# Convolution groups of 16 channels in 8 segments instead of 24 channels in 5, with smaller blocks

## The chip, the core and the metric

The kernel runs on one core of one Trainium2 chip. The metric is device time in microseconds of one execution, lower is better. The engines are TensorE (PE, matmul; PEld is its weight load), VectorE (DVE), ScalarE (ACT), GpSimd (POOL) and SyncE (SP, which here only issues DMAs).

## What is computed

Input x is [8, 4224, 192] float32. First each of 8 heads of 24 channels is convolved causally along the sequence with 7 taps that are a softmax of that head's weights. Then a gated layer follows: a causal depthwise convolution with 5 taps per channel and a sigmoid give the gate, a 192x192 matmul gives the value, and their product goes through a second 192x192 matmul.

```python
out = einsum('hk,bskhg->bshg', softmax(weight), windows of 7 of x)      # x of the next part
gate_pre += conv_w[k] * xp[:, k:k + S, :]                               # k = 0..4
gate = 1 / (1 + exp(-gate_pre))
return gate * (x @ w_val) @ w_out
```

## The kernel before

The 8 sequences are laid end to end as two streams of 4, with padding between them. A step works on a block of the same positions in both streams. Each stream has 16926 positions (columns below), cut into 14 groups and these into 37 steps: 2 steps of 288, 6 of 432, 27 of 482, and a last group of 500 and 244.

**The first convolution** runs on TensorE, for whole groups of steps (`conv_unit`, lines 475 to 494). A window is 64 input positions (`HK`) that give 58 outputs (`HW`). The window's x is the stationary operand, 64 positions by the columns (segment, channel) of one head; the moving operand is the head's banded tap matrix `band`, 64 x 58. A head has 24 channels in 5 segments (`NS`), so M = 120 columns, cut into 64 and 56 (`cut`, line 97). Four matmuls make a pair of windows: two input halves (rows 0 to 63, 64 to 127) by two column halves. `NJS` (line 34) gives the pairs per head and group; in the text such a pair is called a window. Up to `UNIT` windows form a unit, which fills two PSUM banks; `evict` (line 496) has ScalarE copy each bank to the tile `e`, and `scatter` (line 520) then sends each finished head's rows with DMAs into the tiles x1 (channels of chunk 1, 128 of them, both streams side by side) and x2 (the other 64 channels, stream 0 on partitions 0 to 63, stream 1 on 64 to 127). Head h < 5 goes to x1 with one DMA, heads 6 and 7 go to x2 with two, and head 5 is split, with four.

```python
    for r, s in ((0, 0), (1, 1), (0, 1), (1, 0)):
        nc.tensor.matmul(pc[r][64 * s : 64 * s + c1 - c0, k * HW : (k + 1) * HW],
                         lhsT=xtiles[i][p, c + c0 : c + c1], rhs=band[p, 4 * q + hi, :], ...)
to = dst[:, : NS * (b - a)].rearrange("p (s t) -> p s t", s=NS)
dma(to[lo - c0 : hi - c0], e[p : p + NS * (hi - lo), a:b])     # dst is x1[h:120:5] for h < 5
```

**A step** then opens the gate's accumulators in PSUM on ScalarE (line 579: pa for x1, twice the columns; pb for x2), adds four taps to each on VectorE (line 597), and closes them with a sigmoid on ScalarE (line 610). x and the gated product are split into a high and a low part in float32r (`high` line 624, `low` line 629) for the two 192x192 matmuls: `main` (line 666, 128x128, three products), `rows` (line 686), and in plain f32 `columns` (line 695) and `diagonal` (line 653). In the last steps more of it is plain f32 (lines 659 and 678). VectorE multiplies value and gate (line 699; line 725 with a part left to GpSimd). Line 736 copies results to `ot`, and SyncE sends them out.

**Order.** Each engine runs its instructions in program order, and that order is written by hand in `ORDER` (line 116): one string per step whose tokens are the operations above, with +1 or -1 for the next or previous step. c1, c2, c3 are the conv units of the step, e10 to e31 their evictions (with the scatters behind the second), x one load of conv input (line 322) on SyncE's queue, mv/mo the mains, rv/ro the rows, cv/co the columns, dv/do the diagonals. The conv of a group runs two groups ahead of its use (`LAG`). Before the first string a prologue does groups 0 and 1 by other rules (lines 765 to 794). The loads have 8 buffers (`XBUFS`); a load brings 2 heads in small groups and 1 in large ones (`PER_LOAD`). Scatters of the first 3 groups to x2 are issued by GpSimd, two of group 0 by ScalarE, all others by SyncE.

Of the kernel before, what the change touches and what calls it, by code (L numbers as in the profile page):

```python
# [24 lines left out]
NS = 5  # L25
M = NS * HC
# [7 lines left out]
NJS = [2, 3, 3, 3] + [5] * 9 + [3]  # L34
# [10 lines left out]
def second(n):  # L45
    return NS * n * WIN - reach(n)

# [9 lines left out]
BLOCKS = {2: (288, 288), 3: (432, 432), 5: (482, 482, 482)}  # L57
# [3 lines left out]
TAIL = (500, LEFT - 500)  # L61
# [24 lines left out]
PERM = [h * HC + i for i in range(HC) for h in range(5)]  # L86
PERM += [5 * HC + i for i in range(8)]
PERM += [h * HC + i for i in range(HC) for h in (6, 7)]
PERM += [5 * HC + i for i in range(8, HC)]
QUADS = ((6, 7, 5, 0), (1, 2, 3, 4))  # L90
PER_LOAD = {2: 2, 3: 2, 5: 1}

EVEN = 99
SHARE = 241


def cut(g, h):
    return M // 2 if g >= EVEN and h < 5 else 64


UNIT = {2: 4, 3: 6, 5: 7}
# [3 lines left out]
BY_POOL, EARLY, AHEAD = 3, 4, 6  # L105
WARM = 11, 5, 14
# [10 lines left out]
    "rv xh2P+1 x x xl2+1 mv0 xhP+1 mv1 c1 x x x g0 e10 c2 xl+1 g1 A A e11 B A rv+1 dv cv e20 mv0+1 mv1+1 B A",  # L117
    """
    dv phP-1 xh2P+2 B g2-1 B e21-1 sA cv g0 pl-1 c1 g1 sB oA+1 e10 g2 do c2 do-1 e11 xh2+1 oB+1 e20 xh+1 e21 A
    A co co-1 mo0-1 mo1-1 x o2 xl2+2 B A ph o2-1 ph2-1 xl2+1 ph2P  # L120
    """,
    """
    dv A c3-1 B B B sA x x pl2-2 oA+1 cv pl-1 pl2-1 e30-1 e31-1 ro-2 c1 sB o0-2 A g2 A mo1-1 o1-2 mo0-1 oB+1
    e10 B ro-1 e11 rv ph2P o0-1 xh+1 x x xl c2 mv0 e20 o1-1 e21 A xl+1 mv1 B c3 xh2P+2 A sA+1 g0 oA+2 e30 B
    rv+1 g1 B mv1+1 mv0+1
    """,
    "dv do-1 A e31-1 sB xh+1 cv g0 A co-1 c1 x o2-1 oB+1 g2 g1 c2 xl2+1 pl2-1 phP-1 e10 x e11 e20 x x x pl-1",
    """
    dv do-1 ro-2 xl phP-1 ph2-1 e21-1 A B pl2-1 xh2P+1 A sA B B pl-1 oA+1 mo1-2 mo0-2 B o0-2 sB A cv c3-1 g2 A
    A A o1-2 e30-1 oB+1 e31-1 co-1 rv c1 e10 e11 o2-1 sA+1 mv0 mo0-1 mv1 B g0 g1 B mo1-1 xl2+1 xhP+1 ph2 xl+1  # L130
    phP ro-1 c2 oA+2 o1-1 A e20 e21 B do xhP+2
    """,
    """
    dv A B A A cv xh2+1 c3-1 co-1 e30-1 e31-1 rv sB x x o0-2 oB+1 B g2 o2-1 sA+1 mv1 mv0 B g1 pl-1 pl2-1
    xh2P+2 xl2+2 xhP+2 g0 B xl2+1 xl+1 oA+2 ph2P mo0-1 mo1-1 pl2 x x ro-1 o0-1 o1-1 do A
    """,
    """
    dv B A c1-1 e10-1 sB e11-1 co-1 ph-1 cv vp c2-1 e20-1 oB+1 pl-1 A A o2-1 gd mv0 x x e21-1 sA+1 mv1 x x
    oA+2 rv ro-1 gq B mo1-1 mo0-1 g1 B g0 do
    """,  # L140
    """
    dv o1-2 o0-2 B c1-1 co-1 A B cv e10-1 c2-1 sB e11-1 xh2+1 o2-1 xl mv0 vp oB+1 phP-1 e20-1 mv1 A A A xh+1
    pl-1 e21-1 gq ph2P-1 pl2-1 rv gd B sA+1 mo0-1 mo1-1 g0 c1 ro-1 B g1 ph2P pl2 xl2+1 oA+2 e10 e11 c2 o1-1 A
    ph e20 xl+1 B e21
    """,
# [57 lines left out]
    dv e11-1 x x ph-1 c2-1 xh2+1 co-1 e20-1 A A e21-1 x pl2-1 cv sB o2-1 ro-1 pl-1 vp gq rv gd A oB+1 B mv0  # L203
    mo0-1 g0 xh+1 mv1 B xl+1 g1 mo1-1 ph2P sA+1 o0-1 oA+2 B xl2+1 o1-1 c1 do e10 A B
    """,
    """
    dv e11-1 x ph-1 c2-1 xh2+1 co-1 e20-1 A A e21-1 x x pl2-1 cv sB o2-1 ro-1 pl-1 vp gq rv gd A oB+1 B mv0
# [7 lines left out]
    dv e11-1 x x ph-1 c2-1 xh2+1 co-1 e20-1 A A e21-1 x pl2-1 cv sB o2-1 ro-1 pl-1 vp gq rv gd A oB+1 B mv0  # L215
# [3 lines left out]
    dv e11-1 x ph-1 c2-1 xh2+1 co-1 e20-1 A A e21-1 x x pl2-1 cv sB o2-1 ro-1 pl-1 vp gq rv gd A oB+1 B mv0  # L219
# [4 lines left out]
    dv c2-1 co-1 cv o2-1 e20-1 rv pl-1 mv1 mv0 mo0-1 x x x vp e21-1 oB+1 gq gd xh+1 sA+1 g1 mo1-1 ph2P xl2+1  # L224
    pl2 c1 oA+2 e10 B ro-1 g0 B A e11 B xl+1 xh2P+2 o0-1 A
    """,
    """
    dv do-1 ph-1 o1-2 xh+1 c2-1 B e20-1 co-1 cv ro-1 e21-1 o2-1 sB vp oB+1 pl-1 gq rv A A mv0 mv1 B gd g1
# [4 lines left out]
    sA+1 x o0-1 gq B B gd mo1-1 o1-1 oA+2 x mv0 c1 xl+1 ph2P pl2 g1 g0 B e10 B A c2  # L233
# [6 lines left out]
    dv c1-1 cv B A B e10-1 e11-1 vt o1-2 sB oB+1 co-1 xl ro-1 rv A A gp B mo1-1 A o2-1 su+2 B mo0-1 o1-1 mv1  # L240
    mv0 g1 g0
# [20 lines left out]
def kernel(  # L262
# [30 lines left out]
    for g, n in enumerate(NJS):  # L293
        k = PER_LOAD[n]
        order = [h for q in QUADS for h in q]
        for i in range(0, NH, k):
            loads.append((g, order[i : i + k], o))
            o += WK * k * n * M
# [165 lines left out]
    for g, n in enumerate(NJS):  # L464
        for q in range(2):
            ws = [(hi, j) for hi in range(4) for j in range(n)]
            for i in range(0, len(ws), UNIT[n]):
                units.append((g, q, ws[i : i + UNIT[n]]))
    first_unit = [next(i for i, u in enumerate(units) if u[0] == g) for g in range(NG)] + [len(units)]

    def conv_unit(u):
# [479 lines left out]
```

## Time and profile before

| | |
|---|---|
| median of 3 runs | 346.68 us (346.58 to 348.18) |
| the profiled execution | 347.06 us |
| its span, granted clock | 345.3 us, 0.99 |
| busy: PE, DVE, ACT, POOL | 335.5, 316.2, 298.9, 284.4 us |
| DMA | 83.19 MB in 38947 packets, mean 241 GB/s |

The span runs from the first to the last instruction on record; the execution's own time is 1.8 us longer. A matmul's end is modelled, so PE's busy time overstates what the array does; what tells more is the chain that ended last, followed back from the end.

### The profile page before, as it was taken

The numbers are of one execution on the slowest core, as the hardware profiler recorded it, in microseconds if no ns is written. First come the engines' busy times: TensorE is split into PE (matmuls) and PEld (weight loads), VectorE is DVE, ScalarE is ACT, GpSimd is POOL, SyncE is SP. The second block draws the span as 40 slices with busy tenths as digits, with TensorE's granted clock in tenths as the row PEclk, the third lists the DMA queues.
The fourth block names the chain that finished last, engine by engine and source line by source line (L and its number), as shares of the span: only waits on it lengthen the run. The fifth ranks groups of instructions, "written<-read, shape, count | busy, mean of one in ns | idle before, by whom it ended". The sixth has DMA issues, their size and how long they took to land.

```text
span 345.3 us, 13001 instructions
## 1 busy us (share of the span) xinstructions
PE 335.5 (97%) x5334; PEld 215.0 (62%) x5334; DVE 316.2 (92%) x427; ACT 298.9 (87%) x543; POOL 284.4 (82%) x244
## 2 busy tenths in 40 slices
PE   8769999999999999999999999999999999999995
PEld 8755666666666666666666666666666764533343
DVE  4894999999999999999999999999999999999860
ACT  7564978688899999999999999999999999987752
POOL 1988699788999888988888988888989898974461
PEclk9996999999999999999999999999999999999999
DMA  7899969999897897797798897798899675421443
GB/s 265 261 217 280 251 207 285 267 278 321 235 307 270 254 292 257 236 285 265 223 276 284 244 279 274 221 275 285 261 277 324 216 254 153 155 70 56 173 173 132
DMA packets 38947, 83.19 MB, mean 241 GB/s; under 512 B 4936, under 2 KB 17008, under 8 KB 38888
## 3 DMA queue, kind: packets, MB, share of 16 engines
q1 hardware_dynamic: 37440, 80.64, 74.6%
q0 software_dynamic: 896, 1.27, 1.5%
q8 instruction: 42, 0.69, 0.9%
q10 hardware_dynamic: 552, 0.46, 0.4%
q14 instruction: 17, 0.14, 0.1%
HBM read 30.06 MB, written 26.00 MB: 162 GB/s over the span
## 4 chain that ended last, share of the span: by engine, by line
PE 93%; ACT 2%; DMA 1%; SPq 1%; DVE 1%; issue 1%; DVEq 0%
PE p L666 27%; PE p L695 18%; PE p L487 17%; PE p L686 14%; PE p L653 10%; PE p L678 3%; PE p L659 2%; PE p L375 1%; DMA x<-xw 1%; SPq L538 1%; ACT e L503 1%; DVE pa L597 1%; ACT g L610 0%; DVE pb L597 0%; ACT pa L579 0%
## 5 line engine op out<-in xcount | busy, mean ns | idle before, releaser
L597 DVE SCALAR_TENSOR_TENSOR pa<-x,cwt,pa 128x964 f32<-128x964 f32 (+4 forms) x148 | 173.2, 1170 | 2.4 <-ACT pa L579 0.7
L629 POOL TENSOR_TENSOR pl<-g,ph 128x482 fp32r<-128x482 f32 (+5 forms) x67 | 114.6, 1722 | 11.9 <-ACT ph L624 8.6
L629 POOL TENSOR_TENSOR xl<-x,xh 128x964 fp32r<-128x964 f32 (+5 forms) x62 | 98.0, 1584 | 17.1 <-ACT xh L624 12.4
L597 DVE SCALAR_TENSOR_TENSOR pb<-x,cwt,pb 128x482 f32<-128x482 f32 (+4 forms) x142 | 98.3, 692 | 0.7 <-ACT pb L579 0.2
L487 PEld LDWEIGHTS p<-band,x 64*56 64x56 f32 (+1 forms) x3776 | 67.7, 133 | 30.9 <-ACT e L503 8.9
L487 PE MATMUL p<-band,x 64*56 64x58 f32 (+1 forms) x3776 | 73.4, 220 | 4.8 <-issue 1.5
L503 ACT COPY e<-p 120x348 f32<-120x348 f32 (+2 forms) x148 | 63.3, 478 | 9.6 <-PE p L487 8.7
L736 ACT COPY ot<-p 128x482 f32<-128x482 f32 (+4 forms) x111 | 60.1, 550 | 11.7 <-PE p L695 4.0
L699 DVE TENSOR_TENSOR g<-p,g 128x482 f32<-128x482 f32 (+4 forms) x81 | 49.4, 620 | 12.7 <-PE p L695 4.4
L610 ACT ACTIVATE g<-pa 128x964 f32<-128x964 f32 (+4 forms) x37 | 34.8, 942 | 8.5 <-DVE pa L597 6.2
L624 ACT CAST xh<-x 128x964 fp32r<-128x964 f32 (+5 forms) x48 | 39.2, 818 | 0.0
L579 ACT ACTIVATE pa<-x,cwt 128x964 f32<-128x964 f32 (+4 forms) x37 | 38.4, 1037 | 0.7 <-DMA x<-xw 0.2
L653 PE MATMUL p<-g,wof 64*64 64x482 f32 (+4 forms) x148 | 37.3, 556 | 0.0
L653 PE MATMUL p<-x,wvf 64*64 64x482 f32 (+4 forms) x148 | 37.3, 569 | 0.0
L695 PE MATMUL p<-x,wvf 128*64 128x482 f32 (+4 forms) x148 | 36.5, 562 | 0.0
L695 PE MATMUL p<-g,wof 128*64 128x482 f32 (+4 forms) x148 | 36.1, 568 | 0.0
L624 ACT CAST ph<-g 128x964 fp32r<-128x964 f32 (+5 forms) x31 | 29.5, 950 | 0.0
L666 PE MATMUL p<-ph,woh 128*128 128x482 f32 (+4 forms) x74 | 28.8, 389 | 0.0
L624 POOL CAST ph<-g 128x482 fp32r<-128x482 f32 (+6 forms) x36 | 23.5, 653 | 6.2 <-DVE g L699 4.4
L666 PE MATMUL p<-xh,wvh 128*128 128x482 f32 (+2 forms) x64 | 27.5, 429 | 0.0
L666 PE MATMUL p<-pl,woh 128*128 128x482 f32 (+4 forms) x74 | 27.4, 370 | 0.0
L666 PE MATMUL p<-ph,wol 128*128 128x482 f32 (+4 forms) x74 | 27.4, 370 | 0.0
(79 smaller groups left out, 474.3 us busy)
## 6 DMA issues: line engine op xcount, KB each, us to landing
x<-xw SPq DMA_DIRECT2D x72, 300.0 KB
out<-ot SPq DMA_DIRECT2D x27, 723.0 KB
x<-e SPq DMA_DIRECT2D x45, 271.9 KB
x<-xw SPq DMA_DIRECT2D x16, 360.0 KB
x<-e SPq DMA_DIRECT2D x36, 135.9 KB
out<-ot SPq DMA_DIRECT2D x6, 648.0 KB
x<-e SPq DMA_DIRECT2D x20, 163.1 KB
x<-e SPq DMA_DIRECT2D x18, 90.6 KB
```

The source lines that it names most:

```text
L487: nc.tensor.matmul(pc[r][64 * s : 64 * s + c1 - c0, k * HW : (k + 1) * HW], lhsT=xtiles[i][p, c + c0 : c + c1], rhs=band[p, 4 * q + hi, :] ...
L503: nc.scalar.copy(ev[:, a : a + w, r, :], taken["c", u, r][:me, : w * HW].rearrange("p (w t) -> p w t", t=HW))
L579: nc.scalar.mul(acc, views(n, 0)[i], cwt[:, i, 0:1])
L597: nc.vector.scalar_tensor_tensor(out=acc, in0=views(n, k)[i], scalar=cwt[:, i, k : k + 1], in1=acc, op0=ALU.mult, op1=ALU.add,)
L624: copy(two[0], x)
L629: nc.gpsimd.tensor_tensor(out=l, in0=x, in1=h.bitcast(F32), op=ALU.subtract)
L653: nc.tensor.matmul(dst, lhsT=w22, rhs=x[HALVES[r]], start=True, stop=False)
L666: nc.tensor.matmul(acc, lhsT=a[:, r], rhs=b[:, q], start=(fresh and i == 0), stop=(not fresh and i == 2))
L686: nc.tensor.matmul(acc, lhsT=a[p, r], rhs=b[p], start=(fresh and i == 0), stop=(not fresh and i == 2))
L695: nc.tensor.matmul(acc[HALVES[q if what == "v" else 1 - q]], lhsT=w.f[:, W12 : W12 + 64], rhs=x[:, q], start=False, stop=True)
L699: nc.vector.tensor_tensor(out=v, in0=drop("v", n, q), in1=v, op=ALU.mult)
L736: nc.scalar.copy(ots[n][:, q * m : (q + 1) * m], drop("o", n, q))
```

## The change

The 192 channels are put in the order of `HEADS` and cut into 12 groups of 16 channels. A group has 8 segments, so M = 2 x 8 x 8 = 128: its two column halves have 64 columns each, 8 channels by 8 segments, and each half lies in one head, so it has its own `band`. The first 4 groups are chunk 2, the other 8 chunk 1. Group g's channels lie on every 8th partition of x1, or on every 4th of x2, and the weights' rows are permuted to match. A chunk 1 group is scattered with one DMA of 16 channels x 8 segments, a chunk 2 group with two. `NJS` falls to 1, 2 and 3, and the blocks become 230, 462 and 462, with a last group of 482, 482 and 256, 38 steps in all. All units have 6 windows; there are 74 of them, as before. Loads bring 3 groups at once in the small groups and 2 in the large ones, 76 loads instead of 92. In `ORDER` the x tokens are placed anew, most behind an eviction, there is one more string of the steady form, and near the end the unit c2 with its evictions is added in one string; all else stands.

```diff
-NS = 5
-M = NS * HC
+NS = 8
+OCT = 8
+M = 2 * OCT * NS
-NJS = [2, 3, 3, 3] + [5] * 9 + [3]
+NJS = [1, 2, 2, 2] + [3] * 10
-BLOCKS = {2: (288, 288), 3: (432, 432), 5: (482, 482, 482)}
+BLOCKS = {1: (230, 230), 2: (462, 462), 3: (462, 462, 462)}
-TAIL = (500, LEFT - 500)
+TAIL = (482, 482, LEFT - 964)
-PER_LOAD = {2: 2, 3: 2, 5: 1}
+HEADS = (6, 7, 5, 0, 1, 2, 3, 4)
+CHANNELS = [h * HC + i for h in HEADS for i in range(HC)]
+PLACES = [range(g, C2, 4) for g in range(4)] + [range(g, 128, 8) for g in (0, 4, 1, 5, 2, 6, 3, 7)]
+PER_LOAD = {1: 3, 2: 3, 3: 2}
-UNIT = {2: 4, 3: 6, 5: 7}
+UNIT = {1: 6, 2: 6, 3: 6}
...
-    dv e11-1 x x ph-1 c2-1 xh2+1 co-1 e20-1 A A e21-1 x pl2-1 cv sB o2-1 ...
+    dv e11-1 x ph-1 c2-1 xh2+1 co-1 e20-1 A A e21-1 x pl2-1 cv sB o2-1 ...
...
-            two = ((0, cut(g, h)), (cut(g, h), M))
             for r, s in ((0, 0), (1, 1), (0, 1), (1, 0)):
-                p, (c0, c1) = HALVES[r], two[s]
+                p = HALVES[r]
                 nc.tensor.matmul(
-                    pc[r][64 * s : 64 * s + c1 - c0, k * HW : (k + 1) * HW],
-                    lhsT=xtiles[i][p, c + c0 : c + c1],
-                    rhs=band[p, 4 * q + hi, :],
+                    pc[r][HALVES[s], k * HW : (k + 1) * HW],
+                    lhsT=xtiles[i][p, c + 64 * s : c + 64 * s + 64],
+                    rhs=band[p, (2 * h + s) * OCT // HC, :],
...
-        if g < BY_POOL and h >= 5:
+        if g < BY_POOL and h < SMALL:
             dma = nc.gpsimd.dma_start
-        elif g == 0 and h in (3, 4):
+        elif g == 0 and h in BY_ACT:
...
+        def send(dst, a, b):
+            dma(dst[:, : NS * (b - a)].rearrange("p (s t) -> p s t", s=NS), e[:, a:b])
+
+        at = PLACES[h]
+        if h >= SMALL:
+            send(x1[at.start : at.stop : at.step], 0, r)
         else:
+            for i, (a, b) in enumerate(((0, hf), (r - hf, r))):
+                send(x2[64 * i + at.start : 64 * i + at.stop : at.step], a, b)
```

## Rows read from the trace of the kernel before

**Rows 1.** The page: busy us (share of the span) and instructions of each engine.

```profile
PE 335.5 (97%) x5334; PEld 215.0 (62%) x5334; DVE 316.2 (92%) x427; ACT 298.9 (87%) x543; POOL 284.4 (82%) x244
```

**Rows 2.** The chain that ended last: shares of the span by line.

```profile
by line: PE p L666 27.4%; PE p L695 18.5%; PE p L487 16.9%; PE p L686 13.5%; PE p L653 9.8%; PE p L678 3.5%; PE p L659 2.4%; PE p L375 1.4%; DMA x<-xw 1.2%; SPq L538 0.9%; ACT e L503 0.8%; DVE pa L597 0.7%; issue 0.6%; ACT g L610 0.3%; DVE 
```

**Rows 3.** The same chain in order of time: start us, us, what.

```profile
178.41 0.91 PE p L487 x46
...
180.19 0.82 PE p L487 x49
181.01 1.77 PE p L695 x8
182.78 1.63 PE p L686 x12
184.41 2.81 PE p L666 x12
187.22 0.83 PE p L487 x39
188.06 0.83 PE p L653 x7
188.89 0.81 PE p L487 x46
...
195.84 0.91 PE p L487 x47
```

**Rows 4.** Busy us by stretch: the early one, then one steady group of three steps.

```profile
core 0: us, PE busy (x) PEld busy (x) DVE busy (x) ACT busy (x) POOL busy (x), PEclk, DMA share, GB/s
...
20.00:40.00 20.00, 18.11 (x310) 11.33 (x308) 15.41 (x26) 12.68 (x26) 15.21 (x21) 0.83 0.93 244
...
222.25:248.43 26.18, 26.18 (x444) 17.72 (x447) 25.93 (x34) 25.70 (x46) 23.30 (x19) 1.00 0.91 275
```

**Rows 5.** Conv matmuls by shape, whole span: count, busy us, mean ns of one.

```profile
L487 PE MATMUL p<-band,x 64*64 64x58 f32 x1888 | 72.5, 223 | 2.3 <-DMA x<-xw 1.0 <-ACT e L503 0.6 <-ACT pa L579 0.6
...
L487 PE MATMUL p<-band,x 64*56 64x58 f32 x1888 | 66.3, 218 | 2.5 <-issue 1.5 <-ACT e L503 0.8
```

**Rows 6.** TensorE's timeline, successive 128x128 matmuls: start us, us.

```profile
21.09 0.30 PE L666 MATMUL p<-xh,wvh 128*128 128x288 f32 x1
...
21.36 0.29 PE L666 MATMUL p<-xl,wvh 128*128 128x288 f32 x1
...
150.16 0.38 PE L666 MATMUL p<-xh,wvh 128*128 128x482 f32 x1
...
151.25 0.38 PE L666 MATMUL p<-pl,woh 128*128 128x482 f32 x1
```

**Rows 7.** VectorE's taps by shape, and two of them in the timeline.

```profile
L597 DVE SCALAR_TENSOR_TENSOR pa<-x,cwt,pa 128x964 f32<-128x964 f32 x108 | 131.9, 1221 | 1.7 <-ACT pa L579 0.5
...
L597 DVE SCALAR_TENSOR_TENSOR pa<-x,cwt,pa 128x576 f32<-128x576 f32 x8 | 6.5, 817 | 0.1
...
161.68 1.22 DVE L597 SCALAR_TENSOR_TENSOR pa<-x,cwt,pa 128x964 f32<-128x964 f32 x1
162.81 0.71 DVE L597 SCALAR_TENSOR_TENSOR pb<-x,cwt,pb 128x482 f32<-128x482 f32 x1
```

**Rows 8.** The timeline of the start; brackets: idle time before, and what ended it.

```profile
20.95 0.65 ACT L610 ACTIVATE g<-pa 128x576 f32<-128x576 f32 x1 [2.00 <-DVE pa L597]
...
30.49 0.46 DVE L699 TENSOR_TENSOR g<-p,g 128x288 f32<-128x288 f32 x1 [3.56 <-PE p L695]
...
32.06 0.98 ACT L579 ACTIVATE pa<-x,cwt 128x864 f32<-128x864 f32 x1 [0.23 <-DMA x<-xw]
```

**Rows 9.** DMA queues (SyncE's, ScalarE's): packets, MB, share; and SyncE's scatter issues, ns.

```profile
q1 hardware_dynamic: 37440, 80.64, 74.6%
...
q10 hardware_dynamic: 552, 0.46, 0.4%
...
L538 SPq DMA_DIRECT2D x<-e x158: 586/777/1638, 8.4 to 306.3; - x158
```

More of the change, by code (lines that the diff above doesn't have):

```diff
@@ L82 @@
 XC = NS * fifth(NMAX)
[L86 to L90, printed above, removed]
-PER_LOAD = {2: 2, 3: 2, 5: 1}
-EVEN = 99
+HEADS = (6, 7, 5, 0, 1, 2, 3, 4)
+CHANNELS = [h * HC + i for h in HEADS for i in range(HC)]
+C2 = D - 128
+GROUPS = D // (2 * OCT)
+SMALL = C2 // (2 * OCT)
+PLACES = [range(g, C2, 4) for g in range(4)] + [range(g, 128, 8) for g in (0, 4, 1, 5, 2, 6, 3, 7)]
+PERM = [0] * D
+for _g, _p in enumerate(PLACES):
+    for _i, _a in enumerate(_p):
+        PERM[_a + (128 if _g < SMALL else 0)] = CHANNELS[2 * OCT * _g + _i]
+HALF = GROUPS // 2
+PER_LOAD = {1: 3, 2: 3, 3: 2}
 SHARE = 241
-def cut(g, h):
-    return M // 2 if g >= EVEN and h < 5 else 64
-UNIT = {2: 4, 3: 6, 5: 7}
+UNIT = {1: 6, 2: 6, 3: 6}
 XBUFS, EBUFS = 8, 3
@@ L105 @@
 BY_POOL, EARLY, AHEAD = 3, 4, 6
+BY_ACT = GROUPS - 2, GROUPS - 1
 WARM = 11, 5, 14
@@ L294 @@
         k = PER_LOAD[n]
-        order = [h for q in QUADS for h in q]
-        for i in range(0, NH, k):
-            loads.append((g, order[i : i + k], o))
+        for i in range(0, GROUPS, k):
+            loads.append((g, range(i, i + k), o))
             o += WK * k * n * M
@@ L465 @@
         for q in range(2):
-            ws = [(hi, j) for hi in range(4) for j in range(n)]
+            ws = [(hi, j) for hi in range(HALF) for j in range(n)]
             for i in range(0, len(ws), UNIT[n]):
@@ L885 @@
     flat[:, pre : pre + SEQS * PADB].reshape(ns, SEQS, PADB, D)[:, :, :S] = x.reshape(ns, SEQS, S, D)
-    order = [h for q in QUADS for h in q]
+    chunk1, chunk2 = CHANNELS[C2:], CHANNELS[:C2]
     xw, base = [], 0
     for g, n in enumerate(NJS):
-        c = 5 * HC
         win = np.empty((NS * n, 2, HK, D), f)
@@ L897 @@
                 q += base + r * fifth(n)
-                win[w, i, :, c:] = flat[t, q : q + HK, c:]
+                win[w, i, :, :C2] = flat[t, q : q + HK, chunk2].T
         base += TOKS[g]
-        win = win[:, :, ::-1].reshape(NS, n, WK, NH, HC)
-        for i in range(0, NH, PER_LOAD[n]):
-            part = win[:, :, :, order[i : i + PER_LOAD[n]]]
+        win = win[:, :, ::-1].reshape(NS, n, WK, GROUPS, 2 * OCT)
+        for i in range(0, GROUPS, PER_LOAD[n]):
+            part = win[:, :, :, i : i + PER_LOAD[n]]
             xw.append(part.transpose(2, 3, 1, 4, 0).ravel())
     perm = np.array(PERM)
-    taps = weight[order, ::-1]
+    taps = weight[list(HEADS), ::-1]
     bw = np.full((2, HK, NH, HW), -1e30, f)
```

143 lines of the change are left out of this document (63 added, 80 removed).

## The prediction

> **What bounds the kernel now.** I read the page's first parts, then the chain that ended last, then three steady stretches, then single instructions. The page [rows 1] shows three engines near full, TensorE 97%, VectorE 92%, ScalarE 87%, so an average cannot say which one paces. The chain [rows 2] can: nearly all of it is TensorE, and line 487, the convolution, holds 16.9% of 345.3 us, 58.4 us. In order of time [rows 3] the pieces of a step follow each other without a gap: conv, f32 matmuls, rows, mains, conv again. A steady group of three steps takes 26.18 us and TensorE is busy for all of it, VectorE for 25.93, ScalarE for 25.70, the DMA engines for 0.91 [rows 4]. So TensorE paces, with VectorE close behind; a stage gains only by what TensorE's chain loses, and only until VectorE stops it. The exception is the start: there VectorE sits idle for 3.56 us until a TensorE result comes, step 2 opens at 32.06 us [rows 8], and TensorE, after waiting again and again, runs from 20 to 40 us at a mean granted clock of 0.83 [rows 4], so part of that stretch at the lower of its two levels (1.2 and 2.4 GHz).
>
> **The change, part by part.**
> *Convolution windows.* One window is 8 matmuls: two input halves, two column halves, and each f32 matmul runs as two instructions. Before there are 59 windows for each of 8 heads, 472 (3776 matmuls [rows 5] over 8); after, 1 + 3 x 2 + 10 x 3 = 37 for each of 12 groups, 444. The four column and row tiles of a window run side by side, one column half 64 wide and one 56 wide before, both 64 wide after. Does the fuller half cost? The 64-wide matmuls are busy for 72.5 us and the 56-wide for 66.3, equal counts [rows 5]: the narrow tiles finish early and the wide ones set the end, before as after. So a window keeps its price. That price has three readings: 58.4 us over 472 is 0.124 us; conv falls from 0.91 + 0.82 to 0.83 + 0.81 where a step has 13 windows rather than 14 [rows 3], 0.09 us; and the two steps' lengths, 8.81 and 8.62 us from conv to conv, differ by 0.19. I take 0.124, the mean over all of them. Removed: 28 x 0.124 = 3.5 us (2.5 to 5.3), all on the chain. The Trainium skill (TensorE: Matmul & The Clock Gate, LDWEIGHTS) says that a weight load takes time by its columns alone. By the total of columns, 472 x 120 against 444 x 128, that would leave nothing of these 3.5 us and the sum would be +1.4; no run here shows yet whether the column halves load one after the other, and the busy times above speak against it.
>
> *One more step.* Columns in all are the same 16926, cut into 38 steps, not 37, most of 462 columns, not 482. What counts is the part of a step that does not go by columns. Successive 128x128 matmuls start 0.218 us apart at 482 columns (150.16 to 151.25, five of them) and 0.135 apart at 288 (21.09 to 21.36, two) [rows 6]: 0.428 ns a column. A step has 12 passes on line 666 and 6 pairs on line 686; on line 695 eight f32 instructions lie two abreast in 1.77 us [rows 3], 0.44 each, so each counts two passes, 8 in all, and line 653's, four abreast, 4. 30 passes are 12.8 ns a column. A steady step is 26.18 / 3 = 8.73 us; less 482 x 12.8 ns = 6.17 and 13.33 x 0.124 = 1.65 leaves 0.9 us for drains and switches. The added step costs 0.9 us (0, if all went by columns, to 1.45, VectorE's fixed part below).
>
> A steady group then takes 26.18 - 4 x 0.124 - 60 x 12.8 ns = 24.91 us for 1386 columns: 17.97 ns a column against 18.11.
>
> *VectorE and ScalarE.* VectorE's fused tap costs (1221 - 817) / 388 = 1.04 ns per element [rows 7] and a column of a step has 14.5 elements there (four taps of two, four of one, two and a half gate products): 15.1 ns. Its 25.93 us become 25.93 - 60 x 15.1 ns = 25.02, which is more than 24.91. But busy time hides slack: a tap of 1.22 us is followed after 1.13 [rows 7], so each instruction starts up to 0.09 us before the last ends. Start to start, a step is 4 x 1.13, 4 x 0.62 (the 0.71 us tap less 0.09), and an estimated 1.44 for the three gate products by the same slope: 8.4 us, 25.3 a group, and 24.4 after. I count nothing for it; if that slack is not to be had, it is the first rival. ScalarE's evictions stay 148, and 72 of them get 348 columns instead of 406; they lie beside TensorE, on an engine at 25.70 of 26.18 us a group, and shrink with it.
>
> *Scatters.* 13 per group become 16, 182 become 224 in all; loads 92 become 76. ScalarE's queue shows how many engines a scatter uses: 552 packets [rows 9] are two band loads of 128 rows plus 16 closing packets and two scatters of 120 rows plus 12. So 24 channels x 5 segments go over 12 engines while loads go over 16; 16 channels x 8 segments should go over 16. Rows get shorter (2320 to 1392 B, 1160 to 696), packets rise by about 8100. By the count, 8100 x 110 ns (74.6% of 16 engines over 37440 packets) would be 56 us per engine; by bytes nothing. The short packets of ScalarE's queue (40 ns for 0.83 KB, against 110 for 2.15 KB [rows 9]) show that cost goes by bytes, so I count near nothing. SyncE issues 40 scatters more at 0.78 us [rows 9] and 16 loads fewer, GpSimd two more; SyncE has the room, 123 us of 345 for scatters now (158 x 0.777). The loads also move in the written order, most to behind an eviction, so on SyncE's queue they come after that eviction's scatters; their eight buffers hold 16 groups of 12, not 8 heads of 8, so each may come later in its group and I count nothing. The conv of a group runs two groups ahead, some 50 us, and this hides both in steady state; without that cover a wait for a landing would stand at once in the chain, where the loads now have 1.2%.
>
> *The start.* Group 0 shrinks from 576 to 460 columns. If step 2 opens when it does now, the 116 missing columns must be done later at 18.1 ns: +2.1 us. Against it: step 0's taps are shorter by 4 x 0.12 + 2 x 0.06 = 0.6 us, and group 1's last eviction waits for them through ScalarE's order (2.00 us of idling at 20.95 [rows 8]); group 0's conv has 4 windows fewer, 0.5 to 0.7 us; and group 1's scatters leave over more engines. I take +0.5 us, between +2.1 and -0.7, nearer the middle since both the data and VectorE's wait on TensorE come earlier.
>
> *Sum.* -3.5 + 0.9 + 0.5 = -2.1 us against the profiled execution's 347.06 us (span 345.3 and 1.8 around it), 345.0; the median of runs is 0.4 lower, so 344.6 us. A difference of 0.5% (1.7 us) is about what a measurement here can tell from none.
>
> **Rivals.**
> *VectorE paces.* Place: every steady step. For it: 25.93 of 26.18 us busy, and 25.02 against TensorE's 24.91 after. Against: the chain holds next to no VectorE now, and the overlap above. If VectorE keeps the idling it has, a step costs 8.73 - 482 x 15.1 ns = 1.45 us beside its columns, conv gains nothing, and the added step costs 1.45: with the start, 346.68 + 1.45 + 0.5 = 348.6 us, slower. It decides once VectorE's unavoidable time per 462-column step exceeds 24.91 / 3 = 8.30 us (I have 8.1).
>
> *Weight loads share one path.* Then conv goes by columns, 58.4 us stays, and 346.68 + 0.9 + 0.5 = 348.1 us: no change. Against it, rows 5.
>
> *The start gives it back.* Group 1's data is no earlier, the debt of 2.1 us stands: 346.68 - 3.5 + 0.9 + 2.1 = 346.2 us, no change. For it: ScalarE waits a last 0.23 us for a DMA at 32.06 [rows 8], so the data is only just in time.
>
> *The clock.* A mean of 0.83 over 20 us [rows 4] is 6.8 us at the lower level, so 3.4 us lost. If shorter waits at the start keep the clock up all the way, 344.6 - 3.4 = 341.2 us; nothing in the rows says that the waits shrink so far.
>
> *The scatters still use 12 engines.* Then nothing in the sum moves.
>
> **How the numbers follow.** The forecast has 0.55 (own range 342.8 to 346.4), VectorE 0.12, the loads 0.09, the start 0.14, the clock 0.10. Faster by over 0.5% means below 344.95: two thirds of the forecast and the clock, 0.47. Slower, above 348.4, most of VectorE's case and a little beside, 0.13. Between, 0.40. The range reaches from the clock's 341.2 to VectorE's 348.6.
>
> **What would show it.** In the profile after: 3552 matmuls on line 487, all 64*64, and conv of some 1.5 us a step, the same 0.12 us a window (right), or 0.13 and up (loads share a path). Steady groups of 24.9 us with TensorE full; if they take 25.2 or more and TensorE idles before conv or rows on VectorE, the first rival holds. Step 2 should open near 30.5 us; at 32 the start has given back its part. ScalarE's queue should show 2 x (128 + 16) twice, 576 packets. The prediction is wrong if conv's share of the chain does not fall, or if waits for the scattered tiles appear in it.

## The result, and the profile after

The changed kernel takes 349.95 us (median of 14 runs, 347.65 to 350.87) against 346.63 us before (14 runs, 344.5 to 349.11). The ratio is 1.0074, 95% interval [1.0048, 1.0100]: 2.6 us slower, where 2.1 us less were predicted. The profiled execution took 349.12 us, its span 347.3. A second series gave 1.0053 [1.0015, 1.0091] (run e16). Times below are ratios to the kernel before, measured on the same chip, times 346.6 us. The ratios leave out every run that took over 1.5% more than the fastest of its kernel; of the six of e8 below these are four, the profiled one among them.

Line numbers have moved: conv is now line 491 (487 before), eviction 506 (503), scatter 534 (538), x loads 327 (322), taps 587 (597), sigmoid 600 (610), f32 columns 685 (695), mains 656 (666).

First the page's engine line, the chain by line, one steady group of the chain in order of time (start us, us, what), and the busy times of the early stretches and of that group. They answer to [rows 1 to 4].

```profile
PE 332.5 (96%) x5150; PEld 215.6 (62%) x5150; DVE 316.8 (91%) x438; ACT 297.0 (86%) x554; POOL 287.6 (83%) x252
```

```profile
by line: PE p L656 26.1%; PE p L685 17.2%; PE p L491 14.4%; PE p L676 12.8%; PE p L643 9.3%; DMA x<-xw 5.2%; PE p L668 3.4%; PE p L649 2.4%; DVE pa L587 1.6%; DMA x<-e 1.3%; SPq L534 0.9%; issue 0.7%; ACT g L600 0.7%; DVE pb L587 0.6%; SPq 
```

```profile
201.86 0.85 PE p L491 x48
...
203.50 0.69 PE p L491 x48
...
210.16 0.85 PE p L491 x48
...
211.80 0.69 PE p L491 x48
...
218.45 0.85 PE p L491 x48
...
220.13 0.79 PE p L491 x45
```

```profile
20.00:40.00 20.00, 17.05 (x345) 11.42 (x335) 14.58 (x26) 11.98 (x26) 12.89 (x21) 0.83 0.87 237
40.00:60.00 20.00, 18.17 (x328) 11.68 (x330) 18.98 (x25) 15.90 (x32) 17.69 (x15) 1.00 0.77 219
201.86:226.79 24.93, 24.93 (x413) 17.20 (x415) 24.82 (x34) 24.54 (x46) 22.82 (x19) 1.00 0.93 271
```

The first 60 us in one line, the sum of three stretches of 20:

```profile
sum 60.00, PE 49.27 PEld 36.29 DVE 46.88 ACT 39.50 POOL 42.63; mean PE 16.42 PEld 12.10 DVE 15.63 ACT 13.17 POOL 14.21
```

The steady group is what the prediction said: 24.93 us (24.91 forecast), TensorE full, VectorE at 24.82 just under it. The chain shows what is new in this profile: loads of x have gone from 1.2% to 5.2% of it, 4 us to 18 us. A landing of scattered rows, which the prediction named as a sign of being wrong, is in it too (1.3%, a single piece of 4.51 us at 9.85 us); the second profile's chain has no such piece. The third stretch and the same sum of the kernel before (columns as in [rows 4], whose second stretch belongs between) tell where (a second profile of each kernel, in e5 and e16 below, shows how much of it stands):

```profile
40.00:60.00 20.00, 19.85 (x394) 13.14 (x394) 19.32 (x26) 16.82 (x35) 18.81 (x17) 1.00 0.83 252
sum 60.00, PE 53.98 PEld 39.54 DVE 48.70 ACT 42.21 POOL 46.17; mean PE 17.99 PEld 13.18 DVE 16.23 ACT 14.07 POOL 15.39
```

TensorE was busy for 53.98 of the first 60 us before and for 49.27 after: 4.7 us more of idling. The granted clock is the same, a mean of 0.83 in the second stretch, so part of it at the lower level in both. The DMA engines are not busier but idler (0.77 against 0.83 in the third stretch), so it is not that they are full. Here are the changed kernel's waits of TensorE for loads (total us, times, longest), three of them in TensorE's timeline, and the opening of step 2 on ScalarE, which answers to [rows 8]:

```profile
PE p L491 <- DMA x<-xw: 7.7, 7, 1.6
```

```profile
23.06 0.92 PE L491 MATMUL p<-band,x 64*64 64x58 f32 x48 [1.19 <-DMA x<-xw]
...
25.59 1.55 PE L491 MATMUL p<-band,x 64*64 64x58 f32 x48 [1.61 <-DMA x<-xw]
...
54.81 0.92 PE L491 MATMUL p<-band,x 64*64 64x58 f32 x48 [1.27 <-DMA x<-xw]
```

```profile
31.49 1.03 ACT L569 ACTIVATE pa<-x,cwt 128x924 f32<-128x924 f32 x1 [0.22 <-DMA x<-xw]
```

Step 2 opens at 31.49 us, hardly before the 32.06 of [rows 8], with 116 columns less done; the prediction wanted 30.5. (In the second profiles it is 30.80 and, before, 30.59.) The load that TensorE awaits at 54.81 us is issued as late as 50.55 us, between scatters, as SyncE's timeline shows:

```profile
47.65 2.84 SPq L534 DMA_DIRECT2D x<-e  x4
50.55 1.71 SPq L327 DMA_DIRECT2D x<-xw  x2
```

Last, the rows that answer to [rows 5, 9]: conv by shape, the two queues, and SyncE's scatter issues (ns min/median/max).

```profile
L491 PE MATMUL p<-band,x 64*64 64x58 f32 x3552 | 68.7, 222 | 9.5 <-DMA x<-xw 7.7 <-ACT e L506 1.8
```

```profile
q1 hardware_dynamic: 45648, 81.01, 78.2%
...
q10 hardware_dynamic: 576, 0.36, 0.4%
```

```profile
L534 SPq DMA_DIRECT2D x<-e x198: 532/592/2571, 7.7 to 299.1; - x198
```

All 3552 matmuls are 64*64, ScalarE's queue has the 576 packets that the prediction named as the sign of scatters over 16 engines, and a scatter's issue is shorter than before (medians 0.59 us against 0.78).

### The profile page after: what moved, and what is told of

Same layout as the page of the kernel before. It is cut to its first block, busy times and chain, and to the rows that moved or that the text cites. A ratio compares the mean times of both kernels' runs of the same rounds, so it can differ in the third digit from the quotient of the medians.

```text
span 347.3 us, 12737 instructions
## 1 busy us (share of the span) xinstructions
PE 332.5 (96%) x5150; PEld 215.6 (62%) x5150; DVE 316.8 (91%) x438; ACT 297.0 (86%) x554; POOL 287.6 (83%) x252
## 3 DMA queue, kind: packets, MB, share of 16 engines
q1 hardware_dynamic: 45648, 81.01, 78.2%
## 4 chain that ended last, share of the span: by engine, by line
PE 85%; DMA 7%; DVE 2%; ACT 2%; SPq 2%; issue 1%; ACTq 0%
PE p L656 26%; PE p L685 17%; PE p L491 14%; PE p L676 13%; PE p L643 9%; DMA x<-xw 5%; PE p L668 3%; PE p L649 2%; DVE pa L587 2%; DMA x<-e 1%; SPq L534 1%; ACT g L600 1%; DVE pb L587 1%; SPq L327 1%; ACT e L506 1%
## 5 line engine op out<-in xcount | busy, mean ns | idle before, releaser
L587 DVE SCALAR_TENSOR_TENSOR pa<-x,cwt,pa 128x924 f32<-128x924 f32 (+3 forms) x152 | 174.1, 1145 | 3.2 <-ACT pa L569 1.4
L619 POOL TENSOR_TENSOR pl<-g,ph 128x462 fp32r<-128x462 f32 (+4 forms) x69 | 115.3, 1682 | 12.4 <-ACT ph L614 9.1
L619 POOL TENSOR_TENSOR xl<-x,xh 128x924 fp32r<-128x924 f32 (+2 forms) x64 | 99.3, 1556 | 14.9 <-ACT xh L614 13.8
L587 DVE SCALAR_TENSOR_TENSOR pb<-x,cwt,pb 128x462 f32<-128x462 f32 (+3 forms) x146 | 99.3, 680 | 1.9 <-ACT pb L567 1.3
L491 PEld LDWEIGHTS p<-band,x 64*64 64x64 f32 x3552 | 63.9, 135 | 35.1 <-ACT e L506 15.0
L491 PE MATMUL p<-band,x 64*64 64x58 f32 x3552 | 68.7, 222 | 9.5 <-DMA x<-xw 7.7
L506 ACT COPY e<-p 128x348 f32<-128x348 f32 x148 | 60.7, 459 | 13.6 <-PE p L491 13.4
L726 ACT COPY ot<-p 128x462 f32<-128x462 f32 (+3 forms) x114 | 60.6, 540 | 11.2 <-PE p L656 3.6
L689 DVE TENSOR_TENSOR g<-p,g 128x462 f32<-128x462 f32 (+3 forms) x83 | 49.8, 609 | 12.7 <-PE p L685 4.9
L614 ACT CAST xh<-x 128x924 fp32r<-128x924 f32 (+3 forms) x50 | 39.9, 800 | 0.0
```

Source lines behind the costliest of these rows:

```text
L491: nc.tensor.matmul(pc[r][HALVES[s], k * HW : (k + 1) * HW], lhsT=xtiles[i][p, c + 64 * s : c + 64 * s + 64], rhs=band[p, (2 * h + s) * OCT ...
L506: nc.scalar.copy(ev[:, a : a + w, r, :], taken["c", u, r][:, : w * HW].rearrange("p (w t) -> p w t", t=HW))
L587: nc.vector.scalar_tensor_tensor(out=acc, in0=views(n, k)[i], scalar=cwt[:, i, k : k + 1], in1=acc, op0=ALU.mult, op1=ALU.add,)
L614: copy(two[0], x)
L619: nc.gpsimd.tensor_tensor(out=l, in0=x, in1=h.bitcast(F32), op=ALU.subtract)
L689: nc.vector.tensor_tensor(out=v, in0=drop("v", n, q), in1=v, op=ALU.mult)
```

## The experiments

Three theories stood at the outset. Late loads: TensorE waits at the start for loads that SyncE issues later than before. The debt: the smaller first group leaves 116 columns for later. Contention: the scatters' new layout slows the transfers. The added step came up on the way.

**e1, x tokens earlier.** String 0 gets five x tokens in place of one; strings 2 and 3 lose them.

```diff
-"rv xh2P+1 xl2+1 mv0 xhP+1 mv1 c1 g0 e10 c2 xl+1 g1 A A e11 x B A rv+1 dv cv e20 mv0+1 mv1+1 B A",
+"rv xh2P+1 x x xl2+1 mv0 xhP+1 mv1 c1 x x g0 e10 c2 xl+1 g1 A A e11 x B A rv+1 dv cv e20 mv0+1 mv1+1 B A",
```

> The changed kernel with the x tokens of the written order moved forward: five in string 0 instead of one (the loads of group 3 are issued then, as in the kernel before), fewer in strings 2 and 3. Late loads (the theory: what was lost at the start is TensorE waiting for convolution loads that SyncE issues later than before): the wait of 1.27 us for x<-xw at 54.8 us goes, the whole becomes about 1.3 us shorter than the changed kernel, 348.7 us. Debt of the small first group (rival): the wait goes but step times follow the 116 missing columns, within 0.4 us of the changed kernel. Contention of transfers (rival): the earlier loads delay the scatters of group 2, no gain or a loss of up to 1 us.

Measured: 1.0043 [1.0012, 1.0074], 1.1 us less than the changed kernel, and its profile has no wait at 54.8 us. That is what late loads says, but the two intervals overlap, and the changed kernel's own second profile (e16) has no wait there either. So e1 does not settle it.

**e2 and e3, loads of group 2 earlier in the prologue,** alone (e2) and with e1's tokens (e3).

```diff
-            return b + 2 if i < b - 1 else first_load[2]
+            return b + 2 if i < b - 1 else first_load[2] + 2
```

> The changed kernel with the first two loads of group 2 issued as soon as group 0 is convolved, not after the first units of group 1 (one number in the rule for the prologue). Late loads: the waits for x<-xw at 23.06 and 25.59 us (1.19 and 1.61 us) shrink to under 0.5 us together, the whole gains 1 to 2 us against the changed kernel, 348 to 349 us. Debt of the small first group: TensorE's waits only move to VectorE's results of step 0 and 1, gain under 0.4 us. Contention: the two loads (0.8 MB) delay the scatters of groups 0 and 1, step 0 opens later than 17.05 us, no gain.

> Both edits together. Late loads: the gains add up, 2.3 to 3.3 us under the changed kernel, 346.7 to 347.7 us. Debt of the small first group or contention: within 0.5 us of the changed kernel.

Measured: e2 1.0083 [1.0048, 1.0117], no gain; e3 1.0034 [1.0007, 1.0061], hardly different from e1. In e2's profile step 2 opens at 28.02 us rather than 31.49 (30.80 in e16), but step 4 at 49.23 rather than 48.18 (49.25 in e16): what was gained at step 2 is gone two steps on. Late loads was wrong on e2.

**e4, the debt alone.** The kernel before with a first group of 460 columns.

```diff
-BLOCKS = {2: (288, 288), 3: (432, 432), 5: (482, 482, 482)}
+BLOCKS = {2: (230, 230), 3: (432, 432), 5: (482, 482, 482)}
```

> The kernel before with a first group of 230 + 230 columns in place of 288 + 288; the last group takes the 116 more (500 + 360), all else as it was, as many windows and steps. Debt of the small first group: steps 0 and 1 have 116 columns less to do while TensorE waits for data anyway, and these come later at 18.1 ns: slower than before by about 2.1 us, 348.7 us. Late loads (nothing here delays a load): within 0.6 us of before, 346.1 to 347.3 us.

Measured: 1.0022 [0.9991, 1.0052], 0.8 us (-0.3 to 1.8). The full debt of 2.1 us lies outside the interval.

**e5, the kernel before again,** for a second profile.

> The kernel before, unchanged, for a second profile of it: how far TensorE's idle time in the first 60 us, the landing of wv (7.10 us) and the opening of step 0 (16.16 us) vary from one execution to the next. Late loads expects TensorE's idle time within 1 us of the first profile's 9.8 us, and waits for x<-xw on line 487 under 2 us; if the first profile was a lucky one, 1.5 us or more of idle time come on top.

Measured: 1.0014 [0.9977, 1.0050]. Its wait row, and the sum of its first 60 us:

```profile
PE p L487 <- DMA x<-xw: 3.6, 3, 2.9
```

```profile
sum 60.00, PE 51.42 PEld 37.97 DVE 48.67 ACT 42.20 POOL 45.41; mean PE 17.14 PEld 12.65 DVE 16.22 ACT 14.07 POOL 15.14
```

51.42 of 60 us busy, not 53.98, and 3.6 us of waits for loads, not 1.0, at a span of 344.7 us against 345.3. Loads of x are 3.7% of its chain. So single waits of the start differ by some 2.5 us from one execution to the next. The changed kernel's second profile (e16) differs the other way, with 4.6 us of such waits, 5.7% of its chain in loads, and this sum:

```profile
sum 60.00, PE 50.42 PEld 37.50 DVE 46.28 ACT 38.78 POOL 41.49; mean PE 16.81 PEld 12.50 DVE 15.43 ACT 12.93 POOL 13.83
```

Between the second profiles only 1.0 us of the 4.7 read above is left. From here on the ratios decide about the start.

**e6 and e7, two more orders, both on top of e1.** e6 issues a unit's loads ahead of its scatters in the prologue (first diff); e7 loads wv ahead of the third x load (second).

```diff
         for hi in done:
+            i, at = home[g, HALF * q + hi]
+            if at == len(loads[i][1]) - 1 and not by_order:
+                load_x(allowed(i))
+        for hi in done:
             h = HALF * q + hi
-            i, at = home[g, h]
             scatter(g, h, e[:, hi * n * WIN : (hi + 1) * n * WIN])
-            if at == len(loads[i][1]) - 1 and not by_order:
-                load_x(allowed(i))
```

```diff
-    load_x(3)
     load_raw("wv")
+    load_x(3)
```

> Run e1 with one more edit: in the prologue SyncE issues the loads that a finished unit allows ahead of this unit's scatters, not behind them. Late loads: loads 6 and 7 are issued at about 7.8 us rather than 13.0, loads 10 and 11 at about 19.6 rather than 25.4, the waits for x<-xw before 30 us shrink by over 2 us, and the time falls 1 to 2 us under e1 (348.94), to 347 to 348 us. Throughput of the transfers (rival: the DMA engines, at 0.86 of their time in the first 40 us, can't carry loads and scatters any sooner): the scatters land later by what the loads land earlier, step 0 opens after 17.5 us, the time stays within 0.5 us of e1.

> Run e1 with wv loaded ahead of the third convolution load, not behind it. If the decoding of wv and wo on VectorE sets when step 0 opens (woh waits 2.61 us for wof, and step 0 opens right behind it, at 17.05 us): wv lands about 0.8 us earlier, step 0 opens near 16.3 us, and the time falls by 0.4 to 0.8 us under e1 (348.94). If the loads set the start, no change within 0.3 us.

Measured: e6 1.0036 [1.0003, 1.0069], e7 1.0041 [1.0008, 1.0074]; neither can be told from e1. e6 opens step 0 at 19.02 us and the time hardly moves, as the throughput rival said; its profile has 1.8 us of waits for loads, so fewer waits alone did not show in the time either.

**e9, group 0 in units of one load,** on top of e7.

```diff
-UNIT = {1: 6, 2: 6, 3: 6}
+UNIT = {1: 3, 2: 6, 3: 6}
```

> Run e7 with group 0 convolved in four units of three windows, one load each, in place of two units of six that wait for two loads. If the waits of group 0's units for their second load (0.9 to 1.5 us at 8.2 to 8.4 us) hold up the scatters of group 0 and with them the start: the second unit's evictions come a load earlier, step 0 opens near 16.5 us, and the time falls 0.3 to 0.8 us under e7 (348.09). If the start is set by SyncE's issues or by the decoding of the weights, within 0.3 us of e7.

Measured: 1.0019 [0.9985, 1.0054]. Step 0 opens at 16.45 us as expected.

**e11, the reverse of e1.** The kernel before with the changed kernel's late x tokens (string 0 shown, strings 1 and 2 take them up).

```diff
-"rv xh2P+1 x x xl2+1 mv0 xhP+1 mv1 c1 x x x g0 e10 c2 xl+1 g1 A A e11 B A rv+1 dv cv e20 mv0+1 mv1+1 B A",
+"rv xh2P+1 xl2+1 mv0 xhP+1 mv1 c1 g0 e10 c2 xl+1 g1 A A e11 x B A rv+1 dv cv e20 mv0+1 mv1+1 B A",
```

> The kernel before with the x tokens of strings 0 to 2 placed as the changed kernel has them (one, three, four, with two more at the end of string 2 so that string 3 finds as many loads issued); nothing else. Late loads: the loads of group 3 are issued some 15 us later, a wait for x<-xw of about 1 us appears between 45 and 60 us, and the time rises by 0.8 to 1.5 us over the kernel before (346.65). Debt of the small first group alone: no change within 0.3 us.

Measured: 1.0019 [0.9986, 1.0053], 0.7 us (-0.5 to 1.8). In the direction of late loads, but not told from nothing.

**e8 and e12, the layout of the scatters.** e8 puts a group's 16 channels on neighbouring partitions (first added line), e12 puts a chunk 1 group 4 apart within one half (second).

```diff
-PLACES = [range(g, C2, 4) for g in range(4)] + [range(g, 128, 8) for g in (0, 4, 1, 5, 2, 6, 3, 7)]
+PLACES = [range(16 * g, 16 * g + 16) for g in range(4)] + [range(16 * g, 16 * g + 16) for g in range(8)]
+PLACES = [range(g, C2, 4) for g in range(4)] + [range(64 * (g % 2) + g // 2, 64 * (g % 2) + 64, 4) for g in range(8)]
```

> The changed kernel with each group's 16 channels on neighbouring partitions in place of 8 (chunk 1) or 4 (chunk 2) apart; packets, bytes and issues are the same. If the scatters' rows contend for where they are written, the landing of a scatter (5.9 us for 174 KB) grows by 1 us or more, DMA busy time rises above 78.2% of the span on SyncE's queue, and waits for scattered tiles appear. Late loads: the time is set by when loads are issued; if the rows land as before, within 0.5 us of the changed kernel's 349.95.

> The changed kernel with a chunk 1 group's 16 channels 4 partitions apart within one half of the 128 partitions, in place of 8 apart over all. Run e8 (neighbouring partitions) took 384.4 us with SyncE's queue at 90.2% rather than 78.2%. If the landing depends on how many regions of the partitions the 16 engines write to at once, this lies between, nearer the changed kernel: queue share 80 to 84%, time 350 to 356 us. If only neighbouring rows collide, 349.95 within 1 us.

Measured: e8 1.0913 [1.0832, 1.0994], 378.1 us (377.57 and 378.65), with a profile of an execution of 383.42; e12 1.0052 [1.0015, 1.0089], no slower than 8 apart. Of e8, SyncE's queue and two kinds of transfer (KB each, median us to landing); of the changed kernel, the same two; of e12, the queue.

```profile
q1 hardware_dynamic: 45648, 81.01, 90.2%
...
out<-ot SPq DMA_DIRECT2D x33, 693.0 KB, 8.9
x<-e SPq DMA_DIRECT2D x80, 174.0 KB, 9.3
```

```profile
out<-ot SPq DMA_DIRECT2D x33, 693.0 KB, 5.0
x<-e SPq DMA_DIRECT2D x80, 174.0 KB, 5.9
```

```profile
q1 hardware_dynamic: 45648, 81.01, 75.9%
```

Same packets, same bytes, but on neighbouring partitions a scatter takes 9.3 us rather than 5.9, and the output stores that run beside it slow down with it (8.9 us rather than 5.0). So where the rows go matters, and much. That this is what the change lost is not shown: 4 apart in a half brings the queue under its share with 8 apart (75.9% against 78.2%) without a difference in time that can be told.

**e10 and e14, a step more.** e10: one steady group of the changed kernel in four steps. e14: the last group of the kernel before in three. The written order of each has one steady string more.

```diff
+PARTS[8] = (348, 346, 346, 346)
```

```diff
-TAIL = (500, LEFT - 500)
+TAIL = (250, 250, LEFT - 500)
```

> The changed kernel with one steady group of 1386 columns cut into four steps (348 + 346 + 346 + 346) in place of three of 462: as many columns and windows, 39 steps in place of 38. The price of a step by the prediction's sum: 0.9 us, 350.85 us (bounds 0 and 1.45). If a large part of what the change lost is the added step, it costs 2 us or more.

> The kernel before with its last 744 columns in three steps (250 + 250 + 244) in place of two (500 + 244): as many columns and windows, 38 steps in place of 37, the written order one steady string longer, as in the change. The prediction's price of a step: 0.9 us, ratio to the kernel before 1.003. If an added step costs as much as in run e10 (3.2 us more than the changed kernel): ratio 1.007 to 1.010, and the added step is a main part of what the change lost.

Measured: e10 1.0167 [1.0115, 1.0218], 3.2 us over the changed kernel's 1.0074 (1.4 to 5.0 by e10's own interval); e14 1.0092 [1.0057, 1.0127], 3.2 us (2.0 to 4.4). Both are more than three times the 0.9 us of the sum, and e14's whole interval lies above its upper bound of 1.45. For e10 the busy times of two successive stretches, in and behind the short steps (columns as in [rows 4]), and two pieces of the chain there:

```profile
208.20:215.50 7.30, 7.30 (x140) 5.25 (x144) 7.26 (x14) 6.86 (x15) 6.57 (x8) 1.00 0.89 278
215.50:223.50 8.00, 7.79 (x142) 5.83 (x136) 7.96 (x13) 7.76 (x17) 6.44 (x7) 1.00 0.98 302
```

```profile
211.08 3.94 DMA x<-e
...
215.74 3.89 DMA out<-ot
```

VectorE fills these stretches (7.26 of 7.30 us, 7.96 of 8.00), and in the second TensorE begins to idle. VectorE is not alone: the chain leaves TensorE for the landing of scattered rows and of an output store, and the DMA engines are at 0.98. Which of the two sets the price is not shown. For e14, TensorE's pieces of its second step of 250 columns, and the part of the chain ahead of its last matmuls; then the pieces of the step of 500 in the kernel before:

```profile
330.84 0.58 PE p L657 x8
331.42 0.99 PE p L699 x8
332.42 1.04 PE p L663 x4
333.46 1.00 PE p L682 x16
334.46 0.91 PE p L670 x6
...
338.20 0.41 DVE g L703
...
339.49 0.61 issue
340.10 1.27 POOLq L940
```

```profile
324.67 0.99 PE p L653 x5
325.66 1.80 PE p L695 x8
327.46 1.87 PE p L659 x4
329.33 1.81 PE p L678 x16
331.14 1.52 PE p L666 x6
```

On TensorE two steps of 250 take 2 x 4.52 = 9.04 us, one of 500 takes 7.99: a step's fixed part is 1.05 us there, close to the 0.9 of the sum. The rest goes with a stretch from 338.2 to 341.4 us in which the chain leaves TensorE and runs over VectorE, ScalarE and GpSimd's queue; in the kernel before it stays on TensorE from the pieces shown to 341.1 us. Both prices are those of a steady string put in as it stands; whether an order written for the short steps would pay less was not tried.

**e13 and e15, debt and step taken away.** e13: the changed kernel with 924 columns in group 0 and 756 in the last, 444 windows still, 37 steps. e15: with e7's edits too.

```diff
-NJS = [1, 2, 2, 2] + [3] * 10
+NJS = [2, 2, 2, 2] + [3] * 9 + [2]
-TAIL = (482, 482, LEFT - 964)
+TAIL = (500, LEFT - 500)
```

> The changed kernel with two pairs of windows per group of channels in group 0 instead of one: 924 columns first (462 + 462), and 756 last (500 + 256); as many windows in all (444), but 37 steps as in the kernel before, not 38. Small first group and added step: group 0's data and convolution come later (0.8 MB more to load, 12 windows more, steps 0 opens 2 to 6 us later), but 464 columns more are done by then, 8.3 us worth, and a step is saved: 1 to 3 us under the changed kernel, 347 to 349 us. Late loads alone (x tokens and order of loads are unchanged): waits for x<-xw grow with the larger loads, no gain, 349.5 to 352 us.

> Run e13 with run e7's edits too (x tokens of strings 0 to 2 early, wv ahead of the third load). If the three causes (late loads, small first group, added step) add up: 1 to 1.5 us under e13 and no more than the kernel before, 345.5 to 347.5 us. If they stand for the same idle time: within 0.5 us of the better of e13 and e7.

> The changed kernel, unchanged, for a second profile and a ratio beside runs e13 to e15: 1.005 to 1.010 of the kernel before; TensorE's idle time 14 to 15.5 us, waits for x<-xw on line 491 5 to 9 us, step 0 opening between 16.5 and 17.5 us.

Measured: e13 1.0016 [0.9980, 1.0053], e15 1.0020 [0.9991, 1.0050], the changed kernel beside them (e16) 1.0053 [1.0015, 1.0091]. e13 gains 1.3 to 2.0 us, as expected, though its interval overlaps with e16's; e7's edits add nothing to it, so the causes don't simply add up. Its first group opens late, ScalarE waiting for scattered rows (its timeline):

```profile
22.75 1.03 ACT L565 ACTIVATE pa<-x,cwt 128x924 f32<-128x924 f32 x1 [3.90 <-DMA x<-e]
```

So the step that it saves may be partly paid back at the start.

**e17, blocks of 462 and a step more, alone.** The kernel before with these, and 16 windows more since its heads stay in five segments.

```diff
-NJS = [2, 3, 3, 3] + [5] * 9 + [3]
+NJS = [2, 3, 3, 3] + [5] * 10
-BLOCKS = {2: (288, 288), 3: (432, 432), 5: (482, 482, 482)}
+BLOCKS = {2: (288, 288), 3: (432, 432), 5: (462, 462, 462)}
-TAIL = (500, LEFT - 500)
+TAIL = (482, 482, LEFT - 964)
```

> The kernel before with the blocks and the number of steps of the change alone: steady blocks of 462 columns in place of 482, a last group of 482 + 482 + 320 with five pairs of windows per head, 38 steps; heads of 24 channels in 5 segments as before, so 488 windows rather than 472. By the prediction's prices: 16 windows (2.0 us) and a step (0.9 us) more, ratio 1.008. If the added step costs about 3 us (runs e10 and e14): ratio 1.013 to 1.016. The changed kernel has the same blocks with 44 windows less: if regrouping the convolution had no price at the start, it would be 5.5 us under this run; if the start loses 2 to 4 us, 1.5 to 3.5 us under it.

Measured: 1.0196 [1.0138, 1.0254], 6.8 us (4.8 to 8.8). Less 2.0 us for its 16 windows, blocks and step cost 4.8 us, more than even a dear step was to. But the profile also has a pause of TensorE that no wait in the trace accounts for (its chain):

```profile
40.43 3.38 issue
```

So not all of it need come from blocks and step, and its distance from the changed kernel (4.2 us) can't price the start. But its steady groups have the changed kernel's blocks and the old 40 windows. One of three alike (columns as in [rows 4]):

```profile
172.10:197.58 25.48, 25.48 (x442) 17.69 (x441) 25.09 (x34) 24.96 (x47) 22.73 (x19) 1.00 0.91 272
```

**e18, the edits of e9 with the layout of e12.**

> Run e9's edits (x tokens early, wv ahead of the third load, group 0 in units of one load) and run e12's placing (4 apart in one half) together, as the best start found for the changed kernel. Late loads: 1 to 2 us under the changed kernel, ratio to the kernel before 1.000 to 1.004. If e9 and e12 were only scatter of the measurement: 1.004 to 1.007, as the changed kernel.

Measured: 0.9994 [0.9967, 1.0020], the best form of the change, level with the kernel before and 2.8 us under the change as it was made (2.0 us by e16's ratio). The sum of its first 60 us:

```profile
sum 60.00, PE 50.32 PEld 36.76 DVE 48.90 ACT 41.55 POOL 43.78; mean PE 16.77 PEld 12.25 DVE 16.30 ACT 13.85 POOL 14.59
```

TensorE is busy for 50.32 us of the first 60, between the 49.27 and 50.42 of the changed kernel's two profiles, and it waits 6.5 us for loads, between their 7.7 and 4.6. So neither number shows where the gain lies; the columns done, below, do. The four edits touch nothing but the start and where the rows of chunk 1 lie.

## Why the prediction was wrong

**The steady group was right.** 24.91 us forecast, 24.93 measured, TensorE full and VectorE just under. VectorE does not pace there, so the first rival falls for the long steps: its slack was to be had.

**The window's price was right too.** The conv pieces of the group above sum to 4.72 us for 36 windows. Those of the kernel before between 178.41 and 204.56 us sum to 5.05 for 40 (the five of [rows 3], two of 0.02 and the one below). That is 0.08 us per window taken away, but the pieces beside conv get shorter too. The whole group tells more: 25.48 us in e17 with 40 windows, 24.93 with 36 and the same blocks, so 0.14 us a window (0.15 by three groups of each). That lies inside my 0.09 to 0.19. The other part of the gain, 26.18 to 25.48 us for 60 columns, is 11.7 ns a column where I had 12.8.

```profile
197.67 0.73 PE p L487 x42
```

The rival that weight loads share one path falls. A unit of six windows with tiles of 64 and 56 columns takes 0.83 us as the first of a step (187.22 in [rows 3]) and 0.73 as the second (the line above), 1.56 together; with 64 and 64 the two take 0.85 and 0.69, 1.54 together. The Trainium skill (TensorE: Matmul & The Clock Gate, LDWEIGHTS) has the load time go by columns. For single loads the trace agrees in direction (a mean of 129 ns with 56 columns, 137 with 64, in the kernel before), but for a unit, where four tiles run side by side, it shows no such growth.

**Where the change loses, by columns done.** ScalarE's third copy of a step to `ot` (line 736 before, 726 after) tells how many columns are finished. The first lines below come when 4614 and 11844 columns are done before, the second when 4618 and 12010 are done after:

```profile
125.83 0.57 ACT L736 COPY ot<-p 128x482 f32<-128x482 f32 x1
...
257.56 0.57 ACT L736 COPY ot<-p 128x482 f32<-128x482 f32 x1
```

```profile
127.41 0.56 ACT L726 COPY ot<-p 128x462 f32<-128x462 f32 x1
...
260.40 0.55 ACT L726 COPY ot<-p 128x462 f32<-128x462 f32 x1
```

The same marks in the other profiles (in e13 line 722, at 4620 and 12012 columns) cut each span in three:

| | start, us | middle, ns a column | end, us (columns) |
|---|---|---|---|
| before | 125.83 | 18.22 | 87.7 (5082) |
| before again (e5) | 126.04 | 18.13 | 87.6 (5082) |
| changed | 127.41 | 17.99 | 86.9 (4916) |
| changed again (e16) | 129.00 | 17.99 | 86.8 (4916) |
| e18 | 125.12 | 17.99 | 87.0 (4916) |
| e13 | 128.34 | 17.98 | 85.6 (4914) |

The middle is what the prediction said (17.97 against 18.11). The start is 1.6 us late in the first pair and 3.0 in the second. The end takes 2.1 us more than 4916 columns would at the kernel before's 17.25 ns there.

**The step that failed first is the start, "I take +0.5 us".** Less the steady gain of 0.14 ns on each of these 4616 columns, 0.6 us, the forecast has the start about level; it measured 1.6 and 3.0 us late. The +0.5 was built from the debt and from work that becomes shorter. The loads "each may come later in its group and I count nothing" was a gap in it: the cover that I named, conv running two groups ahead, is, by the written order, only being built up at the start. e18, which reorders the start and moves chunk 1's rows, takes 2.0 to 2.8 us off, and by the table all of it before the first mark: its middle and end are the change's. Which edit does it stays open: e1, e6, e7, e9 and the layout of e12 each lie between e18 and the change, and their intervals overlap. The marks can't tell either, since one kernel's start mark differs by 1.6 us between two profiles. That the loads alone are to blame is not shown; e2, which only brings them forward, gained nothing. The rival "the start gives it back" had the right place and the wrong price: its mechanism, the debt, costs 0.8 us (e4), not 2.1.

**The second is the added step, 0.9 us, and with it the end.** A step added to either kernel costs 3.2 us (e10, e14; by the marks above e14's end is 90.5 us, 2.8 longer). My 0.9 was TensorE's own fixed part, and there it is right (1.05); I bounded the rest by VectorE's, and what was left out is that a short step uncovers the chain through the other engines and the DMA queues. The change's own step, with 482 columns in place of 250, is cheaper: e13, with a step and 12 windows fewer in its end, takes 1.3 us less there. The steady gain should have made the end 0.7 us shorter at equal columns and it is 2.1 longer; what makes up the rest of that beside the step stays open.

**The sum, done over.** By the table the start is 1.6 to 3.0 us late, the middle gains 1.0 to 1.7 and the end loses 2.1, which is the 2 to 4 us between the profiles. e18 has the start mended and still stands at -0.2 us, where the forecast has -2.1: the gain of its start and middle is given back at the end.

Contention and 12-engine scatters did not decide: e12 changes the layout and not the time that can be told, and ScalarE's queue shows 16 engines. The clock is not ruled out as a part of the start's loss. Its mean in the second stretch is 0.83 in the first profile of both kernels, but 0.92 before and 0.77 after in the second; over whole runs it is 0.988 in the changed kernel (e16), 0.992 in the kernel before beside it and 0.991 in e18. An estimate from these is 0.004 of 347 us, at most 1.4 us; whether that is a cause of its own or only follows from TensorE's idling, the runs do not show.

## What to carry to other kernels

A gain read from the steady state has to be carried through the start and the end by separate sums, since what covers a transfer or a chain there is not yet, or no longer, running. The price of one more piece is not the busiest engine's fixed part but what a shorter piece uncovers on all the others; add one piece to the old kernel and measure. Compare two profiles by the time at which the same amount of work is done, not by how busy an engine was. And a wait seen in one profile of the start is worth less than it looks: profile the unchanged kernel twice before explaining a difference of 2 us by it.

## What the runs showed of the hardware

Where a scatter's rows go changes its speed: with 16 channels on neighbouring partitions a scatter of 174 KB took 9.3 us and the kernel 1.0913 of the time before, with the same bytes and packets 8 apart 5.9 us and 1.0074. Other transfers slowed with it (stores of the output from 5.0 to 8.9 us). The issue of a scatter on SyncE took 0.59 us (median) for 16 channels by 8 segments and 0.78 us for mostly 24 by 5; whether the number of DMA engines makes the difference or the shape of the rows was not tried. And two profiles of one kernel agree within 0.2 us behind the second mark above, while the start mark of the changed kernel differs by 1.6 us.
